# A decode block on one core: the result held on 32 partitions in blocks of 32 columns instead of on 8 partitions in blocks of 128

## The chip, the cores and the metric

The kernel runs on one core of a Trainium2 chip. The metric is the device time of one execution in microseconds (us). Before the change the median of 3 runs is 1310.18 us (1310.18 to 1310.42).

The engines are named as in the profile: PE (TensorE, matrix products; PEld are its loads of the stationary operand), DVE (VectorE), ACT (ScalarE), POOL (GpSimd) and SP (SyncE, which issues most transfers).

## The reference

One token for each of two sequences goes through a layer norm. The result feeds attention over a cache of 32768 keys and values per head (32 query heads on 8 cache heads) and a gated MLP, and both meet in the output:

```python
def reference(A_x, A_k_cache, A_v_cache, A_wq, A_wo, B_x, B_W_gate, B_W_up, B_W_down):
    ...
    x = A_x                                   # (2, 1, 512)
    xn = _layernorm(x, axis=-1)
    s = _A_ref(xn, A_k_cache, A_v_cache, A_wq, A_wo)
    g = _silu(_B_ref(xn, B_W_gate, B_W_up, B_W_down))
    return x + s * g
```

`_A_ref` projects `xn` with `wq` (512 to 32 x 128), takes softmax(q k) v for each head and projects the 4096 values with `wo` back to 512 columns. `_B_ref` is (relu(xn W_gate) * (xn W_up)) W_down, with 1792 inner columns. Everything is float32. The output is 2 rows of 512 numbers; the caches are 2 x 8 x 32768 x 128 numbers each, 537 MB together, and the profile counts 564.67 MB read.

## The kernel before

There are 16 groups, one for each cache head `hk` of each sequence `b`. A group's 32768 keys are 4 tiles of 8192; tiles are handled in pairs, and one transfer brings a pair (8 MB) of keys or values. Keys go to two buffers `k0` and `k1` in turn, values to `wide`. For each tile DVE transposes the keys in place (`k_transpose`, L656), PE makes scores with the keys as the moving operand (`scores`), DVE takes them out of PSUM with their maximum (L674). When a group's four tiles are there, their maximum is found, ACT takes the exponential (L718), PE and DVE turn the weights round, and PE multiplies them with the values (`values`). `finish_group` then brings a group's 4 heads onto partitions: a product with `heads`, a sum over blocks (`ob`, L783), a 32x32-block transpose (`ot`, L791), and a copy on POOL (L794) that puts the four columns of `ot` into `ots[:, hk, :, b * 16]`.

The order of the work is written out by hand: every operation is recorded by `op` with what it reads and writes, waits follow from that, each engine emits its own in the order of recording, and steps 4 to 64 of PE, DVE and ACT stand as a hardware loop. All matrix products share the helper line L241, all transfers L238, so groups are told apart by the names of their tiles. The transfers of the caches are all issued by SP, in one queue; near its end it issues the last values and then `wo` in ten pieces (`load_wo`): one for each of the heads 0 to 6, and for head 7 a half and two quarters (`wo7_0` with products 0 and 1, `wo7_2`, `wo7_3`). `wo` lies in `k1`.

A float32 matmul of the program stands in the trace as two loads and two matmuls. With a stationary operand of 32 columns, a product fills one group of 32 output partitions, and four matmuls for the four groups run side by side; I call that a round.

`project_near` (L802) multiplies heads 0 to 6 with their rows of `wo`: for each head, four matmuls of 512 columns, whose sums land on the four groups of partitions of `near`. DVE copies `near` to `py_sb` (L821). `project_far` (L823) ends the projection with five products into `far`, in the order j = 0, j = 1, the fold, j = 2, j = 3. Those with a j take a quarter of head 7; the fold multiplies `py_sb` with `fold`, a 0/1 matrix that adds up the four groups. Each is four matmuls of 128 columns, one for each quarter `c` of the 512 result columns, which lands on partitions 32c to 32c + 31. Of those partitions the first is sequence 0 and the 17th is sequence 1, as the row of `ots` has it; the others are zeros. So the result is 4 blocks of 128 columns on 8 used partitions. DVE multiplies by `gy` (L846) and adds `xy` (L848), both on 128x128, and SP stores every 16th partition of `gy` with one transfer.

`gy` is written long before by `mlp_fold`, which folds the MLP's result with four such matmuls and applies Silu on ACT (L644). `xy` is a copy of `x` in the same layout, loaded at the start by a transfer that ACT issues after that of `x` itself.

Of the kernel before, what the change touches and what calls it, by code (L numbers as in the profile page):

```python
# [4 lines left out]
AF = mybir.ActivationFunctionType  # L5
# [3 lines left out]
P = 128  # L9
# [4 lines left out]
NEAR = 7  # L14
ALIGN = 512
PERIOD = 4
APART = 16


class Op:  # L20
# [141 lines left out]
def decode_block_kernel(nc, x, kc, vc, wq, wo, wg, wu, wd, out):  # L162
    B, HKV, SK, DH = kc.shape
    D = x.shape[2]
# [13 lines left out]
    pg = Program()  # L178

    def sbuf(name, *shape, align=32):  # L180
        return nc.alloc_sbuf_tensor(name, list(shape), F32, align_bytes=align)[:]

    def bank(name):
        return nc.alloc_psum_tensor(name, [P, 512], F32)[:]
# [5 lines left out]
    os_ = [sbuf(f"os{i}", P, 512) for i in range(2)]  # L190
# [7 lines left out]
    negone = sbuf("negone", 1, 1)  # L198
    eps_t = sbuf("eps_t", 32, 1)
    zero = sbuf("zero", P, 1)  # L200
    xy = sbuf("xy", P, P)
    gy = sbuf("gy", P, P)
    both = sbuf("both", P, B, NC)
    qd = sbuf("qd", P, REP, B, HKV)
    qall = sbuf("qall", P, B, HKV, 4, REP)
    block_of = sbuf("block_of", P, Q)
    qcur = sbuf("qcur", P, 4, Q)
    ots = sbuf("ots", P, HKV, 4, 32)
    heads = sbuf("heads", P, REP, 32)
    fold = sbuf("fold", P, 32)  # L210
    stat = sbuf("stat", 32, 8)
    mx = sbuf("mx", P, NU)
    ls = sbuf("ls", P, NU)
# [6 lines left out]
    ot = sbuf("ot", P, DH)  # L220
# [5 lines left out]
    ps_d = bank("d")  # L226

    def dve(fn, r=(), w=()):
        pg.op("DVE", fn, r, w)

    def act(fn, r=(), w=()):
        pg.op("ACT", fn, r, w)

    def pe(fn, r=(), w=()):
        pg.op("PE", fn, r, w)

    def load(dst, src, sem, r=(), w=(), engine="SP"):
        pg.op(engine, lambda e: e.dma_start(dst, src), r, w, dma=sem)  # L238

    def mm(out_, lhs, rhs, start, stop):  # L240
        return lambda e: e.matmul(out_, lhs, rhs, start=start, stop=stop, skip_group_check=True)  # L241

    def chain(parts):
        def emit(e):
            for f in parts:
                got = f(e)
            return got

        return emit

    def group(g):
        return g % B, g // B
# [6 lines left out]
    load(wide, wq.rearrange("(p k) n -> p (k n)", k=NKC), "wq", w=["wide"])  # L259

    def of_columns(t):
        return t[0:P:APART, :]

    def by_column(t):
        return t.rearrange("b s (c n) -> c (b s) n", c=4)

    pg.op("POOL", lambda e: e.memset(ident, 0.0), (), ["ident"])
    pg.op(
# [17 lines left out]
    dve(lambda e: e.memset(xy, 0.0), w=["xy"])  # L286
    load(xp[0 : B * APART : APART, :], x.rearrange("b s d -> (b s) d"), "xp", w=["st0"], engine="ACT")
    load(of_columns(xy), by_column(x), "xy", w=["xy"], engine="ACT")
    dve(lambda e: e.memset(perm, 0.0), w=["perm"])
    dve(lambda e: e.memset(mrow, 0.0), w=["mrow"])  # L290
# [4 lines left out]
    for kb in range(4):  # L295
        dve(
            lambda e, kb=kb: e.memset(block_of[Q * kb : Q * kb + Q, kb * REP : (kb + 1) * REP], 1.0),
            w=["block_of"],
        )
    dve(lambda e: e.memset(heads, 0.0), w=["heads"])  # L300
    dve(lambda e: e.memset(o_ps, 0.0), w=["o"])
    dve(lambda e: e.memset(ots, 0.0), w=[f"ots{hk}" for hk in range(HKV)])

    dve(
        lambda e: e.tensor_reduce(
# [20 lines left out]
    n = 1  # L326
    while n < Q:
# [18 lines left out]
    dve(  # L346
        lambda e: e.tensor_copy(both, ident.rearrange("p (c k) -> p k c", c=NC)[:, 0 : B * APART : APART, :]),
        ["ident"],
# [5 lines left out]
        ["ident"],  # L354
        ["fold"],
    )

    dve(lambda e: e.reduce_sum(stat[:, 0:1], xp, axis=AX.X), ["st0"], ["stat"])
    dve(lambda e: e.tensor_scalar_mul(stat[:, 1:2], stat[:, 0:1], 1.0 / D), ["stat"], ["stat"])
# [71 lines left out]
    WO, WOK = {}, {}  # L431
# [192 lines left out]

    def mlp_fold():
        dve(lambda e: e.tensor_copy(os_[0], ps_d), ["d"], ["os0"])
        pe(
            chain(
                [
                    mm(  # L630
                        ps_d[32 * c : 32 * c + 32, :P],
                        fold,
                        os_[0][:, c * P : (c + 1) * P],
                        True,
                        True,
                    )
                    for c in range(4)
                ]
            ),
            ["fold", "os0"],  # L640
            ["d"],
        )
        act(
            lambda e: e.activation(gy, ps_d[:, :P], AF.Silu, bias=zero, scale=1.0),  # L644
            ["d", "zero"],
            ["gy"],
        )
# [127 lines left out]
    def finish_group(g):  # L775
        b, hk = group(g)
        pe(
            mm(ps_m[1], heads.rearrange("p h m -> p (h m)"), os_[0], True, True),
            ["heads", "os0"],
            ["m1"],  # L780
        )
        dve(
            lambda e: e.reduce_sum(  # L783
                ob.rearrange("p (j q) -> p q j", j=4),
                ps_m[1].rearrange("p (c q j) -> p q j c", c=NC, j=4),
                axis=AX.X,
            ),
            ["m1"],
            ["ob"],
        )  # L790
        dve(lambda e: e.transpose(ot, ob), ["ob"], ["ot"])  # L791
        pg.op(
            "POOL",
            lambda e: e.tensor_copy(ots[:, hk, :, b * APART], ot.rearrange("p (j m) -> p j m", j=4)[:, :, 0]),  # L794
            ["ot"],
            [f"ots{hk}"],
        )

    near, far = ps_s
    py_sb = os_[0]  # L800

    def project_near(hks):  # L802
        for hk in hks:
            pe(
                chain(
                    [
                        mm(
                            near[32 * j : 32 * j + 32, :],
                            ots[:, hk, j, :],
                            WO[hk][:, j, :],  # L810
                            hk == 0,
                            hk == NEAR - 1,
                        )
                        for j in range(4)
                    ]
                ),
                [f"ots{hk}", WOK[hk][0]],
                ["s0"],
            )
        if hks[-1] == NEAR - 1:  # L820
            dve(lambda e: e.tensor_copy(py_sb, near), ["s0"], ["os0"])  # L821

    def project_far(hks):  # L823
        parts = []
        for hk in hks:
            for j in range(4):
                parts.append((ots[:, hk, j, :], WO[hk][:, j, :], [f"ots{hk}", WOK[hk][j]]))
        parts.insert(2, (fold, py_sb, ["fold", "os0"]))
        for n, (o, w, held) in enumerate(parts):
            pe(  # L830
                chain(
                    [
                        mm(
                            far[32 * c : 32 * c + 32, :P],
                            o,
                            w[:, c * P : (c + 1) * P],
                            n == 0,
                            n == len(parts) - 1,
                        )
                        for c in range(4)  # L840
                    ]
                ),
                held,
                ["s1"],
            )
        dve(lambda e: e.tensor_mul(gy, far[:, :P], gy), ["s1", "gy"], ["gy"])  # L846
        dve(
            lambda e: e.tensor_add(gy, gy, xy),  # L848
            ["gy", "xy"],
            ["gy"],  # L850
        )
# [6 lines left out]
    for j in range(PAIRS + 2):  # L858
        s, v = 2 * j, 2 * (j - 2)
# [22 lines left out]
        if j == 1:  # L882
            mlp_fold()
        if ends:
            if live:
                tile_maximum()
            if summed:
                sums()
            if live:
                maximum()  # L890
            if summed:
                take_o()
                if not live:
                    project_near(range(1))
                finish_group(j // 2 - 1)
# [14 lines left out]
            load_wo()  # L910

    project_near(range(1, NEAR))
    project_far(range(NEAR, HKV))
    load(by_column(out), of_columns(gy), "out", r=["gy"])

    sems = {s: nc.alloc_semaphore(f"sem_{s}") for s in pg.count}
# [55 lines left out]
```

## Time and profile before

| | before |
|---|---|
| median of 3 runs | 1310.18 us |
| the profiled execution | 1310.07 us |
| its span | 1308.4 us |
| mean granted clock of TensorE | 0.833 |
| PE busy | 846.4 us (65%) |
| DVE busy | 706.8 us (54%) |
| moved by DMA | 564.79 MB, mean 432 GB/s |

A row of the timeline has the start and the time taken in us, the engine, the line, the operation, what it writes and reads, the shapes and how many were merged into the row; in brackets stands how long the engine was idle before it and what ended that. Instructions of one row can overlap, so the time of a row is not the sum of its members. A row of the page's groups ends with the busy time in us, the mean of one instruction in ns, and the idle time before them with what ended it.

### The profile page before, as it was taken

How to read it: one execution, taken by the hardware profiler on the slowest of the kernel's cores; microseconds unless marked ns; L12 is line 12 of the kernel's file. 1: busy time of each engine (PE TensorE's matmuls, PEld its weight loads, DVE VectorE, ACT ScalarE, POOL GpSimd, SP SyncE). 2: the span in 40 equal slices, each digit the busy share in tenths (PEclk: the TensorE clock that was granted, in tenths of full speed). 3: DMA queues.
4: the chain of work that ended last, by engine and by line, in shares of the span. 5: the costliest groups of instructions: out<-in, count | busy, mean ns of one | idle time of the engine just before them, and what ended most of it. 6: DMA issues, size and time to landing. Idle time of an engine off the chain costs nothing.

```text
span 1308.4 us, 10823 instructions
## 1 busy us (share of the span) xinstructions
PE 846.4 (65%) x4624; PEld 198.9 (15%) x4624; DVE 706.8 (54%) x642; ACT 51.4 (4%) x133; POOL 10.3 (1%) x38
## 2 busy tenths in 40 slices
PE   3566675675566577556667657666666766765676
PEld 1111111111111111111111111111111111111121
DVE  3566554565655465664546665455665545656521
ACT  0001000000000000000000000000000000000000
POOL 0000000000000000000000000000000000000000
PEclk9678788978878897887898787789877879888788
DMA  9999999999999999999999999999999999999998
GB/s 417 421 434 443 437 427 443 427 437 429 439 427 439 429 439 441 427 443 429 437 429 439 427 439 429 439 441 427 443 429 437 429 439 427 439 429 439 441 427 360
DMA packets 11268, 564.79 MB, mean 432 GB/s; under 512 B 1258, under 2 KB 1274, under 8 KB 1660
## 3 DMA queue, kind: packets, MB, share of 16 engines
q1 hardware_dynamic: 11244, 564.67, 99.7%
q8 instruction: 6, 0.10, 0.0%
q14 instruction: 2, 0.02, 0.0%
q10 hardware_dynamic: 16, 0.01, 0.0%
HBM read 564.67 MB, written 0.00 MB: 432 GB/s over the span
## 4 chain that ended last, share of the span: by engine, by line
DMA 64%; DVE 18%; PE 14%; issue 4%; SPq 0%
DMA k<-in_A_k_cache_dram 59%; DVE k L656 18%; PE o L241 8%; PE s L241 5%; DMA k<-in_A_wo_dram 3%; DMA w<-in_A_wq_dram 2%; PE m_ps L241 1%; SPq L238 0%; PE m_ps L689 0%; DVE gy L846 0%; DVE gy L848 0%
## 5 line engine op out<-in xcount | busy, mean ns | idle before, releaser
L241 PE MATMUL s<-k,qcur 128*32 128x512 f32 x2048 | 497.7, 694 | 398.1 <-DVE k L656 397.7
L656 DVE STREAM_TRANSPOSE k<-k 128x2048 f32<-128x2048 f32 x256 | 565.2, 2275 | 171.4 <-DMA k<-in_A_k_cache_dram 171.4
L241 PE MATMUL o<-w,wt 128*16 128x512 f32 x1984 | 245.3, 596 | 7.4 <-DMA w<-in_A_v_cache_dram 7.4
L241 PEld LDWEIGHTS s<-k,qcur 128*32 128x32 f32 x2048 | 88.3, 121 | 804.7 <-DVE k L656 665.0
L733 DVE STREAM_TRANSPOSE wt<-pt 128x512 f32<-128x512 f32 x64 | 45.4, 709 | 133.0 <-PE pt L241 129.6
L674 DVE TENSOR_SCALAR_CACHE_REDUCE st<-s 128x512 f32<-128x512 f32 x64 | 43.0, 672 | 118.1 <-PE s L241 118.1
L718 ACT ACTIVATE st<-st,nb 128x512 f32<-128x512 f32 x64 | 45.4, 710 | 1110.6 <-DVE nb L715 1110.6
L241 PEld LDWEIGHTS o<-w,wt 128*16 128x16 f32 x1984 | 62.7, 98 | 165.5 <-issue 165.5
L241 PE MATMUL pt<-st,perm 128*128 128x512 f32 x128 | 66.6, 645 | 1.5 <-ACT st L718 1.5
L759 DVE RECIPROCAL rl<-m_ps 128x1 f32<-128x1 f32 x16 | 2.7, 168 | 109.3 <-PE m_ps L241 109.3
L241 PEld LDWEIGHTS pt<-st,perm 128*128 128x128 f32 x128 | 25.0, 206 | 41.4 <-issue 37.2
L241 PE MATMUL m_ps<-os,heads 128*128 128x512 f32 x32 | 20.1, 715 | 13.7 <-DVE os L763 13.7
L783 DVE TENSOR_REDUCE ob<-m_ps 128x128 f32<-128x512 f32 x16 | 11.1, 693 | 21.6 <-PE m_ps L241 21.6
L241 PE MATMUL m_ps<-w,wt 128*32 128x512 f32 (+1 forms) x128 | 16.0, 632 | 7.9 <-DMA w<-in_A_wq_dram 7.9
L526 POOL TENSOR_TENSOR qcur<-qall,block_of 128x128 f32<-128x128 f32 x16 | 6.5, 406 | 1019.0 <-PE s L241 984.8
L241 PE MATMUL o<-k,wt 128*16 128x512 f32 x64 | 10.0, 792 | 4.0 <-DMA k<-in_A_v_cache_dram 4.0
L241 PE MATMUL m_ps<-negone,mrow 1*128 1x1 f32 x32 | 6.0, 256 | 9.3 <-DVE mrow L704 9.3
L718 ACT ACTIVATION_READ_ACCUMULATOR st<-st,nb 128x1 f32 x64 | 11.9, 186 | 0.0
L763 DVE SCALAR_TENSOR_TENSOR os<-o,rl,own 128x512 f32<-128x512 f32 x16 | 11.9, 743 | 0.0
L477 DVE COPY os<-m_ps 128x512 f32<-128x512 f32 x2 | 1.4, 691 | 15.9 <-PE m_ps L241 15.9
L385 PE MATMUL m_ps<-ident,st 32*128 32x32 f32 x4 | 0.7, 307 | 14.2 <-DVE st L374 14.2
L241 PE MATMUL s<-k,ots 128*32 128x512 f32 (+1 forms) x88 | 8.1, 481 | 1.6 <-DMA k<-in_A_wo_dram 1.6
(79 smaller groups left out, 94.9 us busy)
## 6 DMA issues: line engine op xcount, KB each, us to landing
k<-in_A_wo_dram SPq DMA_DIRECT2D x7, 1024.0 KB, 36.2
w<-in_B_W_gate_dram SPq DMA_DIRECT2D x1, 3584.0 KB, 20.0
w<-in_B_W_up_dram SPq DMA_DIRECT2D x1, 3584.0 KB, 28.1
w<-in_B_W_down_dram SPq DMA_DIRECT2D x1, 3584.0 KB, 15.7
k<-in_A_k_cache_dram SPq DMA_DIRECT2D x32, 48.6
k<-in_A_wo_dram SPq DMA_DIRECT2D x1, 512.0 KB, 42.9
k<-in_A_wo_dram SPq DMA_DIRECT2D x2, 256.0 KB, 26.4
w<-in_A_v_cache_dram SPq DMA_DIRECT2D x31, 29.6
```

Of the source, the lines that this page charges most:

```text
L241: return lambda e: e.matmul(out_, lhs, rhs, start=start, stop=stop, skip_group_check=True)
L385: lambda e, k=k: e.transpose(px[:, k * 32 : (k + 1) * 32], xquad[:, k, :], ident[:32, :32])
L477: dve(lambda e, q=qs, h=half: e.tensor_copy(q, pq[h]), [f"m{half}"], [f"os{half}"])
L526: lambda e: e.tensor_tensor(qcur.rearrange("p e (k h) -> p e k h", h=REP), qall[:, b, hk].unsqueeze(2).to_broadcast([P, 4, Q // REP, REP]) ...
L656: dve(lambda e: e.transpose(at_, at_), [f"k{t // 2 % 2}"], [key])
L674: lambda e: e.tensor_scalar(st[u], ps_s[t % 2], SCALE, None, op0=ALU.mult, op1=ALU.max, accum_out=mx[:, u : u + 1],),
L718: lambda e, u=u: e.activation(st[u], st[u], AF.Exp, bias=nb, scale=1.0, accum_out=ls[:, u : u + 1]),
L733: dve(lambda e: e.transpose(wt[t % 2], ps_p[t % 2]), [f"pt{t % 2}"], [f"wt{t % 2}"])
L759: dve(lambda e: e.reciprocal(rl, ps_m[1][:, :1]), ["m1"], ["rl"])
L763: lambda e: e.scalar_tensor_tensor(os_[0].rearrange("p (c d) -> p c d", c=NC), o_ps.rearrange("p (c d) -> p c d", c=NC), rl, own.unsqueeze ...
L783: lambda e: e.reduce_sum(ob.rearrange("p (j q) -> p q j", j=4), ps_m[1].rearrange("p (c q j) -> p q j c", c=NC, j=4), axis=AX.X,),
```

## The change

The result's 512 columns become 16 blocks of 32 (`PARTS`), one on every fourth partition in pairs: block c of sequence b lies on partition 8c + 4b. `xy` and `gy` are 128x32. To get there, each product of the end is 16 matmuls of 32 columns (`spread_mm`): block 4a + i goes to the group a of 32 partitions, with a stationary operand for each i whose used column is 8i + 4b and whose other columns are zero; the four i of a group add up on the same 32x32 field. Those four stationary operands stand in `folds` for the fold and in `last` for head 7, each filled by copies that write one value to four places (`spot`): two on DVE for `folds` at the start, and four on POOL for each of the two groups of head 7 in the place of one. `ots` holds heads 0 to 6 alone. The load of `xy` and the store have 32 runs of 32 numbers where they had 8 of 128.

```diff
+    WIDTH = D // PARTS
+    xy = sbuf("xy", P, WIDTH)
+    gy = sbuf("gy", P, WIDTH)
...
-    ots = sbuf("ots", P, HKV, 4, 32)
+    ots = sbuf("ots", P, HKV - 1, 4, 32)
+    folds = sbuf("folds", P, 4, 32)
+    last = sbuf("last", P, 4, 4, 32)
...
     def of_columns(t):
-        return t[0:P:APART, :]
+        return t[0 : P : P // (B * PARTS), :]
+
+    def spot(t, b):
+        step = P // (B * PARTS)
+        flat_ = t.rearrange("p i m -> p (i m)")
+        return flat_[:, b * step : b * step + 3 * (32 + B * step) + 1 : 32 + B * step]
+
+    def spread_mm(t, lhs, rhs, start, stop):
+        return [
+            mm(
+                t[32 * a : 32 * a + 32, :WIDTH],
+                lhs[:, i, :],
+                rhs[:, (4 * a + i) * WIDTH : (4 * a + i + 1) * WIDTH],
+                start and i == 0,
+                stop and i == 3,
+            )
+            for i in range(4)
+            for a in range(4)
+        ]
 
     def by_column(t):
-        return t.rearrange("b s (c n) -> c (b s) n", c=4)
+        return t.rearrange("b s (c n) -> c (b s) n", c=PARTS)
...
-    dve(lambda e: e.memset(ots, 0.0), w=[f"ots{hk}" for hk in range(HKV)])
+    dve(lambda e: e.memset(ots, 0.0), w=[f"ots{hk}" for hk in range(HKV - 1)])
+    dve(lambda e: e.memset(last, 0.0), w=["last"])
+    dve(lambda e: e.memset(folds, 0.0), w=["folds"])
...
+    for b in range(B):
+        dve(
+            lambda e, b=b: e.tensor_copy(
+                spot(folds, b), fold[:, b * APART : b * APART + 1].to_broadcast([P, 4])
+            ),
+            ["fold"],
+            ["folds"],
+        )
...
     def mlp_fold():
         dve(lambda e: e.tensor_copy(os_[0], ps_d), ["d"], ["os0"])
...
+        pe(chain(spread_mm(ps_d, folds, os_[0], True, True)), ["folds", "os0"], ["d"])
         act(
-            lambda e: e.activation(gy, ps_d[:, :P], AF.Silu, bias=zero, scale=1.0),
+            lambda e: e.activation(gy, ps_d[:, :WIDTH], AF.Silu, bias=zero, scale=1.0),
...
+        row = ot.rearrange("p (j m) -> p j m", j=4)[:, :, 0]
+        if hk < HKV - 1:
...
+        else:
+            for j in range(4):
+                pg.op(
+                    "POOL",
+                    lambda e, j=j: e.tensor_copy(
+                        spot(last[:, j], b), row[:, j : j + 1].to_broadcast([P, 4])
+                    ),
+                    ["ot"],
+                    ["last"],
+                )
...
-    def project_far(hks):
...
+    def project_far():
+        hk = HKV - 1
+        parts = [(last[:, j], WO[hk][:, j, :], ["last", WOK[hk][j]]) for j in range(4)]
+        parts.insert(2, (folds, py_sb, ["folds", "os0"]))
+        for n, (lhs, w, held) in enumerate(parts):
+            pe(chain(spread_mm(far, lhs, w, n == 0, n == len(parts) - 1)), held, ["s1"])
+        dve(lambda e: e.tensor_mul(gy, far[:, :WIDTH], gy), ["s1", "gy"], ["gy"])
```

The end of PE's order shows the five products. The names are the output, the moving operand and the stationary one; the sizes are those of the output. Before:

```order
L241 MATMUL s<-k,ots 32x512 x24
L241 MATMUL s<-k,ots 32x128 x8
L241 MATMUL s<-os,fold 32x128 x4
L241 MATMUL s<-k,ots 32x128 x8
L917 UNCONDITIONAL_BRANCH
```

With the change:

```order
L245 MATMUL s<-k,ots 32x512 x24
L245 MATMUL s<-k,last 32x32 x32
L245 MATMUL s<-os,folds 32x32 x16
L245 MATMUL s<-k,last 32x32 x32
L929 UNCONDITIONAL_BRANCH
```

Of each product's four matmuls there are now sixteen, with a quarter of the columns each, 80 where there were 20; the order of the products stays. POOL's order ends, before:

```order
L526 TENSOR_TENSOR qcur<-qall,block_of 128x128
L794 COPY ots<-ot 128x4 x3
L917 UNCONDITIONAL_BRANCH
L941 ISA
```

and with the change:

```order
L813 COPY ots<-ot 128x4
L821 COPY last<-ot 128x4 x8
L929 UNCONDITIONAL_BRANCH
L953 ISA
```

The last two of the sixteen copies of `ot` have become eight.

More of the change, by code (lines that the diff above doesn't have):

```diff
@@ L17 @@
 APART = 16
+PARTS = 16
 class Op:
@@ L200, in decode_block_kernel @@
     zero = sbuf("zero", P, 1)
-    xy = sbuf("xy", P, P)
-    gy = sbuf("gy", P, P)
+    WIDTH = D // PARTS
+    xy = sbuf("xy", P, WIDTH)
+    gy = sbuf("gy", P, WIDTH)
     both = sbuf("both", P, B, NC)
@@ L626, in mlp_fold @@
         dve(lambda e: e.tensor_copy(os_[0], ps_d), ["d"], ["os0"])
[L627 to L642, printed above, removed]
+        pe(chain(spread_mm(ps_d, folds, os_[0], True, True)), ["folds", "os0"], ["d"])
         act(
-            lambda e: e.activation(gy, ps_d[:, :P], AF.Silu, bias=zero, scale=1.0),
+            lambda e: e.activation(gy, ps_d[:, :WIDTH], AF.Silu, bias=zero, scale=1.0),
             ["d", "zero"],
@@ L791, in finish_group @@
         dve(lambda e: e.transpose(ot, ob), ["ob"], ["ot"])
[L792 to L797, printed above, removed]
+        row = ot.rearrange("p (j m) -> p j m", j=4)[:, :, 0]
+        if hk < HKV - 1:
+            pg.op(
+                "POOL",
+                lambda e: e.tensor_copy(ots[:, hk, :, b * APART], row),
+                ["ot"],
+                [f"ots{hk}"],
+            )
+        else:
+            for j in range(4):
+                pg.op(
+                    "POOL",
+                    lambda e, j=j: e.tensor_copy(
+                        spot(last[:, j], b), row[:, j : j + 1].to_broadcast([P, 4])
+                    ),
+                    ["ot"],
+                    ["last"],
+                )
     near, far = ps_s
@@ L821, in project_near @@
             dve(lambda e: e.tensor_copy(py_sb, near), ["s0"], ["os0"])
-    def project_far(hks):
[L824 to L846, printed above, removed]
+    def project_far():
[5 more added lines that the diff above has]
+        dve(lambda e: e.tensor_mul(gy, far[:, :WIDTH], gy), ["s1", "gy"], ["gy"])
         dve(
@@ L912, in decode_block_kernel @@
     project_near(range(1, NEAR))
-    project_far(range(NEAR, HKV))
+    project_far()
     load(by_column(out), of_columns(gy), "out", r=["gy"])
```

## The prediction

> **What bounds the kernel now.** I read the page first, for what limits the whole span.
>
> ```profile
> span 1308.4 us, 10823 instructions
> PE 846.4 (65%) x4624; PEld 198.9 (15%) x4624; DVE 706.8 (54%) x642; ACT 51.4 (4%) x133; POOL 10.3 (1%) x38
> DMA  9999999999999999999999999999999999999998
> GB/s 417 421 434 443 437 427 443 427 437 429 439 427 439 429 439 441 427 443 429 437 429 439 427 439 429 439 441 427 443 429 437 429 439 427 439 429 439 441 427 360
> q8 instruction: 6, 0.10, 0.0%
> DMA 64%; DVE 18%; PE 14%; issue 4%; SPq 0%
> L241 PE MATMUL s<-k,qcur 128*32 128x512 f32 x2048 | 497.7, 694 | 398.1 <-DVE k L656 397.7
> L241 PEld LDWEIGHTS s<-k,qcur 128*32 128x32 f32 x2048 | 88.3, 121 | 804.7 <-DVE k L656 665.0
> L241 PEld LDWEIGHTS o<-w,wt 128*16 128x16 f32 x1984 | 62.7, 98 | 165.5 <-issue 165.5
> L241 PEld LDWEIGHTS pt<-st,perm 128*128 128x128 f32 x128 | 25.0, 206 | 41.4 <-issue 37.2
> ```
>
> The reader is to see that the transfers are busy in every slice but the last, at 417 to 443 GB/s. Nothing the change does there touches a transfer of the caches, so only what stands behind the last transfer, or holds one up, can move the end. PE has 398 us in which it waits for the transposed keys: work added to it in the middle falls into that. Then I read the timeline of the end, after the last pieces of `wo` have been asked for, and the chain of waits over the same stretch.
>
> ```profile
> 1261.28 42.93 DMA k<-in_A_wo_dram
> ...
> 1304.35 1.62 PE s L241 x40
> ...
> ```
>
> ```profile
> 1304.15 0.69 DVE L821 COPY os<-s 128x512 f32<-128x512 f32 x1 [5.73 <-PE s L241]
> 1304.32 0.41 PEld L241 LDWEIGHTS s<-k,ots 128*32 128x32 f32 x16 [1.15 <-issue]
> 1304.35 0.65 PE L241 MATMUL s<-k,ots 128*32 128x128 f32 x16 [0.27 <-DMA k<-in_A_wo_dram]
> 1304.89 0.16 PEld L241 LDWEIGHTS s<-os,fold 128*32 128x32 f32 x8 [0.17 <-DVE os L821]
> 1304.89 0.42 PE L241 MATMUL s<-os,fold 128*32 128x128 f32 x8
> 1305.03 0.24 PEld L241 LDWEIGHTS s<-k,ots 128*32 128x32 f32 x8
> 1305.13 0.79 PE L241 MATMUL s<-k,ots 128*32 128x128 f32 x16
> 1305.50 0.16 PEld L241 LDWEIGHTS s<-k,ots 128*32 128x32 f32 x8 [0.23 <-DMA k<-in_A_wo_dram]
> 1305.99 0.29 DVE L846 TENSOR_TENSOR gy<-s,gy 128x128 f32<-128x128 f32 x1 [1.15 <-PE s L241]
> 1306.32 0.29 DVE L848 TENSOR_TENSOR gy<-gy,xy 128x128 f32<-128x128 f32 x1
> 1306.64 0.69 SPq L238 DMA_DIRECT2D out_dram<-gy  x1
> ```
>
> The end is a relay. The last piece of `wo` lets PE start at 1305.50; PE is done at 1305.13 + 0.79 = 1305.92; DVE multiplies and adds until 1306.61; the store is issued at 1306.64 and the span ends at 1308.4, 1.76 us later. Within this, three waits matter: the first piece of the last head (1304.32), DVE's copy of the near sum (1304.89), and the last piece (1305.50). A matmul of the program stands as two loads and two matmuls in these rows (x8 for the fold's four), so PE goes through five products of 8, 40 in all, and each product is two rounds of four, one for each group of 32 output partitions.
>
> **The change part by part.** DVE: L846 and L848 go from 128 columns to 32.
>
> ```profile
> 11.74 0.68 DVE L365 TENSOR_TENSOR st<-st 32x512 f32<-32x512 f32 x1
> 1295.13 0.17 DVE L759 RECIPROCAL rl<-m_ps 128x1 f32<-128x1 f32 x1 [15.84 <-PE m_ps L241]
> ```
>
> 512 columns take 0.68 us and 128 take 0.29: 0.39 / 384 = 1.0 ns a column. So 96 columns less are 0.097 us, twice that 0.19. The floor is not reached: a single column out of PSUM takes 0.17, and 0.29 - 0.10 = 0.19 is still above. By that floor the two can give between 0.19 and at most 0.24; I take **-0.19**. It is on the path in full, since the store waits for it.
>
> PE at the end: each product becomes 8 rounds of four (16 matmuls, two passes) with 32 moving columns, where it was 2 rounds with 128. The moving columns per group of partitions are the same in all, so the question is what one short round costs. Three bounds from rows:
>
> ```profile
> 1297.65 0.13 PEld L241 LDWEIGHTS s<-k,ots 128*32 128x32 f32 x4 [0.30 <-issue]
> 1298.08 0.13 PEld L241 LDWEIGHTS s<-k,ots 128*32 128x32 f32 x4 [0.30 <-issue]
> 31.68 1.95 PE L241 MATMUL pt<-both,os 128*128 128x8 f32 x16
> 1295.00:1303.00 8.00, 6.65 (x51) 1.66 (x51) 1.93 (x4) 0.00 (x0) 0.19 (x1) 1.00 1.00 419
> 1303.00:1308.40 5.40, 2.64 (x48) 1.09 (x48) 1.28 (x3) 0.00 (x0) 0.00 (x0) 1.00 0.24 93
> ```
>
> Streaming: rounds of 512 columns follow each other by 0.43 us, so 32 columns stream in 0.027. The loads of the weights run under it (each set of four starts with the round before). Loading: with 8 moving columns and 128 columns of weights, 16 pairs take 1.95, (1.95 - 0.26) / 15 = 0.113 each, so the load sets the pace there; mean loads of 98, 121 and 206 ns for 16, 32 and 128 columns give about 1 ns a column, so 32 columns are about 0.031. Issue: the fold's eight loads take 0.16 in all with about 0.11 each, so they start within 0.05, some 7 ns apart with the matmuls between them; four pairs need 0.027. The last two rows are stretches of the end, whose columns after the interval are the time busy of PE, its loads, DVE, ACT and POOL, then the granted clock (1.00), the share of DMA and GB/s: no throttle enters. The greatest of the three is 0.031 a round. The last product is then 8 x 0.031 = 0.25 where it is 0.22: **+0.03**. The products ahead of it: 16 rounds from 1304.35 are over by 1304.85, before the fold may start (1304.89); 16 more from there by 1305.39, before the last piece (1305.50). That cover is good up to (1305.50 - 1304.89) / 16 = 0.038 a round; above it PE, not the last transfer, is late. Below, a round cannot be cheaper than 0.027, which gives +0.00. Above, nothing in the trace runs pairs denser than four per 0.11, and that end is rival one.
>
> The Trainium skill speaks against this edit. "TensorEngine Tiling (Array Packing)", section Performance Considerations (Instruction Overhead), has a matmul of few moving columns cost as much as one of 60, some 60 cycles, and says not to take the tiling out of a dimension that is already small. If the floor holds for each group of columns by itself, its 25 ns at 2.4 GHz lie under the 27 ns of the stream and change nothing; rows 7 ns apart agree with that. If it held across the groups, 160 x 25 ns = 4.0 us would stand where 40 short rounds do, the result of rival one within half a microsecond.
>
> The store has 32 runs of 128 bytes where it had 8 of 512.
>
> ```profile
> 0.74 0.39 SPq L238 DMA_DIRECT2D w<-in_A_wq_dram  x1
> 2.65 0.60 ACTq L238 DMA_DIRECT2D xy<-in_A_x_dram  x1
> w<-in_A_wq_dram SPq DMA_DIRECT2D x1, 21.9
> ```
>
> Its issue took 0.69, the load of `xy`, which has the same shape, 0.60, and a load over 128 partitions 0.39. If more partitions make the issue that much shorter, the store ends 0.30 sooner. On the other side, the 8.39 MB of `wq` landed 21.9 us after issue; at 432 GB/s they move in 19.4, so a transfer over all partitions has up to 2.5 us around its data, 0.7 more than the store's 1.76. The nearest row is the store itself (same queue, same 4 KB): I take **0.00**, between -0.30 and +0.7. "DMA: Bandwidth & Descriptors" of the skill, section Specifications, has writes under 512 bytes read and modify memory first, which speaks for the dear end; no run shown here has such a store.
>
> Edits that I cost at nothing, with their cover:
>
> ```profile
> 1298.48 0.19 POOL L794 COPY ots<-ot 128x4 f32<-128x4 f32 x1 [36.28 <-DVE ot L791]
> 10.35 0.67 DVE L358 TENSOR_REDUCE stat<-st 32x1 f32<-32x512 f32 x1 [3.54 <-DMA st<-in_A_x_dram]
> 2.74 0.48 DVE L301 MEMSET o<- 128x512 f32 x1
> ```
>
> The last head's row goes out as four POOL copies, one after the other: 4 x 0.19 and a wait between, under 2 us from 1298.48, needed at 1304.32; without cover 0.6 or so. At the start DVE gets one more such memset of 128x512, one of a quarter of that, and two copies of four columns: less than 1.2 if each of these three costs a half of the 0.48, before a wait of 3.54 for `x`. The fold of the second block, near 102 us, is 8 rounds for 2: at 0.109 each +0.65, in the stretch where PE waits for keys. The load of `xy` on ACT's queue is read first by work that waits for far later transfers.
>
> Sum: -0.19 + 0.03 + 0.00 = **-0.16 us**. The profiled execution took 1310.07 (span 1308.4 and 1.67 around it), so 1309.91; it lies 0.11 under the median of the runs, so I forecast 1310.0.
>
> **The rivals.** One, on the other side: short pairs go no faster than the densest that the trace shows, four per 0.109. PE then needs 40 rounds from 1304.35; the last starts at 1304.35 + 39 x 0.109 = 1308.60 and ends 0.28 later, 2.96 us after today's 1305.92. Less DVE's 0.19 that is +2.77: 1312.9. It decides from 0.038 a round. For it: no row has shorter rounds, and nowhere does a group of partitions get its next weights so soon. Against it: loads start 7 ns apart, and the pace of every long round is explained by its columns. A milder form has loads and streams one after the other, 0.027 + 0.027 = 0.055: last start 1306.50, end 1306.78, +0.86 - 0.19 = +0.67: 1310.8.
>
> Two: the store is dearer by up to 0.7, or the longer code hurts: 72 more matmuls of four instructions each, and the page has six instruction packets of 0.10 MB, 16 KB each; one that falls on a DMA engine with the last piece holds it for 16 KB / (432 / 16 GB/s) = 0.6 us. Either way 1310.6 or so.
>
> Three: the store over more partitions is issued sooner: -0.16 - 0.30, 1309.7.
>
> Four: the change does not do what it says, if DVE's operations have a floor near today's 0.29. The 0.17 of a single column speaks against it; the time would be 1310.2.
>
> **How the numbers follow.** Forecast 0.50, rival one 0.10 and its milder form 0.13, two 0.13, three 0.11, four 0.03. The range takes in three at its low end with 0.3 for a median's scatter, and rival two and the mild form at the high end: 1309.4 to 1311.3; left out are rival one and the outer parts of the others. A fifth of a percent, 2.6 us, is about what a measurement of this kernel can tell from no change: rival one lies at that bound, so slower gets 0.06 of its 0.10, and 0.02 for a hold-up that I have not seen; no case gains 2.6 us, so faster 0.02; within, 0.90.
>
> **What would show it.** Right: L846's and L848's successors at 0.19 each and 0.2 us less between PE's end and the store's issue; short rounds 0.03 apart, so that PE still waits for the last piece of `wo` before its last 32 loads. Wrong: the last product's loads starting late with no transfer as their releaser (rival one), a longer stretch from the store's issue to the span's end (two), a last piece that lands late beside an added instruction packet, or a first scores row that comes later than before, where the start was not hidden.

## The result and the profile after

| | before | changed |
|---|---|---|
| median of 22 runs each | 1310.21 us (1310.01 to 1310.57) | 1312.13 us (1311.80 to 1312.59) |
| ratio | | 1.0015, 95% interval 1.0009 to 1.0021 |
| profiled execution, its span | 1310.07 and 1308.4 us | 1311.80 and 1310.3 us |
| mean granted clock | 0.833 | 0.836 |

The change costs 1.9 us; the forecast was 1310.0, with 1309.4 to 1311.3 as the range. These are the rows of the changed kernel's timeline at the end, from the first piece of `wo` for head 7 on:

```profile
1304.32 0.67 PEld L245 LDWEIGHTS s<-k,last 128*32 128x32 f32 x64 [1.19 <-issue]
1304.35 0.74 PE L245 MATMUL s<-k,last 128*32 128x32 f32 x63 [0.31 <-DMA k<-in_A_wo_dram]
1304.89 0.39 PEld L245 LDWEIGHTS s<-os,folds 128*32 128x32 f32 x32
...
1305.19 0.68 PEld L245 LDWEIGHTS s<-k,last 128*32 128x32 f32 x64
...
1305.21 0.76 PE L245 MATMUL s<-k,last 128*32 128x32 f32 x62
1307.79 0.19 PE L245 MATMUL s<-k,last 128*32 128x32 f32 x1 [1.83 <-issue]
1308.02 0.19 DVE L858 TENSOR_TENSOR gy<-s,gy 128x32 f32<-128x32 f32 x1 [3.23 <-PE s L245]
1308.24 0.19 DVE L860 TENSOR_TENSOR gy<-gy,xy 128x32 f32<-128x32 f32 x1
1308.46 0.66 SPq L242 DMA_DIRECT2D out_dram<-gy  x1
```

The 80 matmuls of the program at the end are 160 in the trace. All but one of them are through by 1305.21 + 0.76 = 1305.97, as the forecast has it. The last one alone starts at 1307.79. Its weights are loaded (the 64 loads end at 1305.87), its piece of `wo` was there for the 31 before it, and the trace knows no semaphore that it waited for: `issue`. The chain of waits over the same stretch says the same, and its 1.83 us of `issue` are the only wait that the chain before does not have:

```profile
1304.35 1.62 PE s L245 x108
1305.96 1.83 issue
1307.79 0.20 PE s L245
1308.00 0.02 issue
1308.02 0.20 DVE gy L858
```

The sum from the two timelines: PE ends at 1307.98 where it ended at 1305.92, +2.06. From there to the store's issue it is 0.48 where it was 0.72, -0.24. From the issue to the span's end 1.84 where it was 1.76, +0.08. Together +1.90, the span's difference.

What the last matmul lacks shows in the page's list of DMA queues, where the queue q8 carries instructions. The changed kernel has

```profile
q8 instruction: 7, 0.11, 0.0%
q10 hardware_dynamic: 52, 0.01, 0.0%
```

where the kernel before has six packets. Each is 16 KB. Their places in time are in the trace, though no row of a view prints them; these are the last ones of q8, in us from the span's start, with the time that the packet took:

```
before   1293.07  0.96
after    1289.30  0.88
after    1305.36  0.93
```

The seventh packet starts while PE is in its last products and is moved by 1306.28; the last matmul goes 1.5 us later. That the packet holds the last matmul's code is so far a guess from this order in time; the experiments test it.

### The profile page after: what moved, and what is told of

Its sections match the earlier page's. It is cut to its first block, busy times and chain, and to the rows that moved or that the text cites. A ratio compares the mean times of both kernels' runs of the same rounds, so it can differ in the third digit from the quotient of the medians.

```text
span 1310.3 us, 11121 instructions
## 1 busy us (share of the span) xinstructions
PE 843.9 (64%) x4768; PEld 199.5 (15%) x4768; DVE 707.2 (54%) x646; ACT 51.3 (4%) x133; POOL 11.4 (1%) x44
## 4 chain that ended last, share of the span: by engine, by line
DMA 63%; DVE 18%; PE 14%; issue 4%; SPq 0%
DMA k<-in_A_k_cache_dram 58%; DVE k L673 18%; PE o L245 8%; PE s L245 5%; DMA k<-in_A_wo_dram 3%; DMA w<-in_A_wq_dram 2%; PE m_ps L245 1%; SPq L242 0%; PE m_ps L706 0%; DVE gy L858 0%; DVE gy L860 0%
## 5 line engine op out<-in xcount | busy, mean ns | idle before, releaser
L245 PEld LDWEIGHTS m_ps<-w,wt 128*32 128x32 f32 x128 | 5.9, 123 | 17.1 <-issue 17.1
```

## The experiments

The theory A from this: PE runs code out of blocks of 16 KB, and asks for one more when it enters a block. The products at the end are 160 pairs of load and matmul; a block holds 128 pairs. The last matmul is the first instruction of a block, the request for it goes out only in the first two products, and the 128 pairs ahead of it are through in 1.4 us. "Runtime: NRT & Kernel Launch" of the Trainium skill, section "Instruction fetch mechanics", describes such blocks, of 16 KiB or 256 instructions, and calls the cost of crossing into one mostly hidden; the packets here have that size, and the cost is not hidden.

The rivals: B, the array or PSUM holds back the last short matmul; C, each instruction more costs; and, after the first four runs, D, a boundary near the end costs its 2 us whatever runs ahead of it. To move the boundaries and nothing else at the end, matmuls are added to (or one is taken from) PE's code long before, near 100 us, where PE waits for keys. Each matmul is two pairs, so n of them move every later boundary by 2n pairs.

**e1: one matmul less.**

```diff
-                    for i in range(FI)
+                    for i in range(FI) if i != 5
```

> The changed kernel, with one of the 14 matmuls of the MLP's down projection left out (its part of the inner columns is missing from the result), near 90 us. The end of the program is as in the changed kernel; all of PE's code behind that place moves four instructions towards the start. Theory A (the last matmul's code comes late: it is the first instruction of a 16 KB block that PE's sequencer asks for only when it enters the block before, and the 128 pairs of that block are gone through faster than the block arrives): the last matmul falls into the block before, its idle time of 1.83 us is gone, PE ends near 1306.0, time 1310.1. Rival B (the last matmul waits for something in the array or PSUM: a drain of the short rounds, the sums that pile up on one field): nothing at the end differs, so 1312.1 with the same idle time. Rival C (every instruction more costs): 4 of 288 less, 1312.1.

Measured: 1309.99 us (1309.83 to 1310.24, 11 runs; before 1310.14 beside it). The end of its timeline:

```profile
1305.60 0.68 PEld L245 LDWEIGHTS s<-k,last 128*32 128x32 f32 x64
...
1305.62 0.77 PE L245 MATMUL s<-k,last 128*32 128x32 f32 x63
1306.46 0.19 DVE L858 TENSOR_TENSOR gy<-s,gy 128x32 f32<-128x32 f32 x1 [1.25 <-PE s L245]
```

The end has the same instructions on the same data paths, and the last matmul is no longer late. B falls: four instructions that were left out 1200 us earlier cannot change what the array does at the end. C falls as well, since 4 of 288 instructions took 2.1 us with them.

**e2, e3, e4: 8, 16 and 24 matmuls more.** The MLP's fold repeats itself; the sums written first are overwritten. The diff is e2's; e3, e4 and later e5, e6, e9 and e10 have another number in the place of 8.

```diff
-        pe(chain(spread_mm(ps_d, folds, os_[0], True, True)), ["folds", "os0"], ["d"])
+        once = spread_mm(ps_d, folds, os_[0], True, True)
+        pe(chain((once + once)[:8] + once), ["folds", "os0"], ["d"])
```

> The changed kernel, with the MLP's fold made longer by 8 matmuls whose sums are written over at once (near 102 us, result unchanged). The end of the program is the same; its code lies 16 pairs further on. Theory A: 16 pairs of the last product and the last matmul stand in the late block, which is asked for about 15 pairs after the start of the five products instead of 31, 0.1 us sooner; the rest then takes 17 pairs x 0.008 and the idle time shrinks little: between 1312.0 and 1312.3, with the idle time now ahead of a group of about 17 pairs. Rival B: 1312.1, idle before the last matmul alone. Rival C: 1312.2.

> As before with 16 matmuls more in the MLP's fold (result unchanged). Theory A: the block is entered with the last pair of head 6, which waits for its piece of wo at 1303.0 instead of 1304.45; 3.3 us later, at 1306.3, its first instruction can go, 33 pairs follow: PE ends near 1306.8, time about 1310.9. Rival B: 1312.1. Rival C: 1312.3.

> As before with 24 matmuls more in the MLP's fold (result unchanged). Theory A: the block is entered within head 5 or sooner, near 1301, so it is there by 1304.4 and nothing waits for it: no idle time but that for the last piece of wo, 1310.1, with 96 instructions more than the changed kernel. Rival B: 1312.1. Rival C: 1312.4 or more.

Measured: e2 1312.18 us (1311.83 to 1312.64), e3 1312.97 (1311.11 to 1313.48), e4 1309.98 (1309.80 to 1310.34), 11 runs each. The place of the wait, in e2's timeline and then in e3's:

```profile
1305.26 0.62 PE L245 MATMUL s<-k,last 128*32 128x32 f32 x46
1308.09 0.34 PE L245 MATMUL s<-k,last 128*32 128x32 f32 x17 [2.21 <-issue]
```

```profile
1305.46 0.46 PE L245 MATMUL s<-k,last 128*32 128x32 f32 x30
1307.88 0.46 PE L245 MATMUL s<-k,last 128*32 128x32 f32 x33 [1.95 <-issue]
```

The reader is to see x17 and x33 behind the wait where the changed kernel has x1: two pairs for each matmul added, exact. The wait sits on a place of the code, not on a piece of work. In e4 there is none:

```profile
1304.68 0.74 PE L245 MATMUL s<-k,last 128*32 128x32 f32 x63 [0.46 <-DMA k<-in_A_wo_dram]
...
1305.54 0.77 PE L245 MATMUL s<-k,last 128*32 128x32 f32 x63
1306.38 0.19 DVE L859 TENSOR_TENSOR gy<-s,gy 128x32 f32<-128x32 f32 x1 [1.39 <-PE s L245]
```

Its packet of instructions starts at 1301.76, and 96 instructions more than in the changed kernel make it 2 us faster. e3 missed its number: 3 of 11 runs lie at 1311.1 to 1311.2, near the 1310.9 expected, and 8 at 1312.6 to 1313.5. The near ones are partly luck: their spans are 1308.9 to 1309.1, about 0.6 us above the median of e6's, 1308.4, and the rest is the 2.0 to 2.2 us that these executions took outside the span, where e6's took about 1.5. In the profiled one, a long one, the packet starts at 1305.48, not near 1304.

**e5: 18 more, to get a wait of half the length.**

> As e3, with 18 matmuls more in the MLP's fold (result unchanged). Theory A, with what e1 to e4 showed (some 3.4 us from the entry into a block to the first instruction of the next one): the block is entered in the middle of head 6's matmuls, which wait for their piece of wo until about 1303.1. The next block's first instruction can go near 1306.5; 37 pairs and the pipeline follow, PE ends near 1307.0, one us later than without a wait: 1311.0, in every run, between the changed kernel's 1312.1 and e4's 1310.0. Rival D (a block boundary anywhere in the last stretch costs its 2 us whole, or nothing): 1312.2 or 1310.0.

Measured: 1312.51 us, again in two clumps: 3 of 11 runs at 1310.5 to 1310.9, 8 at 1312.2 to 1313.0. The profiled one, a long one, has x37 behind a wait of 2.27 us, as counted, and its packet starts at 1305.68. Only the short executions come near the 1311.0 expected; neither A as written nor D tells why there are two kinds.

**e6: 40 more, the best version.**

> The changed kernel with 40 matmuls more in the MLP's fold (result unchanged). Theory A: the block that holds the last 81 pairs is asked for at the entry into the one before, 209 pairs from the end, near 1295; nothing waits, and 160 instructions more near 102 us cost nothing: 1310.0, no idle time of PE in the last products but that for the last piece of wo.

Measured: 1309.94 us (1309.85 to 1310.17, 11 runs) beside 1310.15 (1309.95 to 1310.48, 33 runs) of the kernel before; ratio 0.9999 with an interval of 0.9990 to 1.0008, so the comparison itself does not set the two apart. The packet starts at 1296.55, with the entry expected near 1295. The end of its timeline:

```profile
1305.18 0.68 PEld L245 LDWEIGHTS s<-k,last 128*32 128x32 f32 x64
...
1305.20 0.77 PE L245 MATMUL s<-k,last 128*32 128x32 f32 x63
1306.04 0.19 DVE L859 TENSOR_TENSOR gy<-s,gy 128x32 f32<-128x32 f32 x1 [1.19 <-PE s L245]
1306.27 0.19 DVE L861 TENSOR_TENSOR gy<-gy,xy 128x32 f32<-128x32 f32 x1
1306.48 0.66 SPq L242 DMA_DIRECT2D out_dram<-gy  x1
```

**e7: the kernel before, with its last matmul moved to the start of a block, by the count of instructions.**

```diff
-                    for c in range(4)
+                    for c in (0, 1, 2, 3) * 3
```

> The kernel before, with its MLP fold done three times (8 matmuls more, result unchanged). By the count of instructions its last matmul then stands first in its block, as in the changed kernel. Theory A: the block before it holds 128 pairs of which the last 40 alone are the far products, so it is entered near 1293 and the last block is there 10 us before its use: 1310.2, no idle time ahead of the last matmul. Rival D: 1312.1.

Measured: 1310.20 us (1310.05 to 1310.91), the kernel before beside it 1310.15. The last products follow their piece of `wo` as in the kernel before:

```profile
1305.21 0.77 PE L241 MATMUL s<-k,ots 128*32 128x128 f32 x16
1305.56 0.16 PEld L241 LDWEIGHTS s<-k,ots 128*32 128x32 f32 x8 [0.21 <-DMA k<-in_A_wo_dram]
```

Its last packets start at 1289.84 and at 1305.87. The kernel before has none after 1293.07, so here PE entered one more block near its end; that this block begins with the very last matmul rests on the count alone. D falls: a boundary at the end costs nothing where the 128 pairs ahead of the last matmul, counted back from the end, take some 14 us.

**e8: half as far, 8 blocks of 64 columns.**

```diff
-PARTS = 16
+PARTS = 8
```

The helpers' numbers of four follow it (`PARTS // 4` fields to a group).

> The change with 8 blocks of 64 columns on 16 partitions: 8 matmuls of 64 columns a product. DVE's last two operations at 0.23 each, 0.13 less together; rounds of 0.055; the store has 16 runs of 256 bytes. By the count of instructions the last block starts 32 pairs before the end and the one before is entered near 1294. Theory A: nothing late, 1310.0 to 1310.1. Rival C (what counts is the number of matmuls): 1310.9.

Measured: 1310.16 us (1310.05 to 1310.49), the kernel before 1310.15. DVE's two operations take 0.22 each, no wait of PE for its code. So A holds to within 0.1 us and C, with 1310.9, does not. The packets that had to be there in time started at 1289.84 in e7 and at 1291.66 in e8, where the expectations had the blocks entered near 1293 and 1294, so the count tells the time of a request to some 3 us and not better. In the profiled execution the store is issued 0.58 us after PE's end, where it was 0.72 before, as expected; the medians do not show this 0.14, which is less than the runs of one kernel scatter.

**e9 to e12: when is a block asked for?**

> As e5, with 20 matmuls more in the MLP's fold (result unchanged): the block before the last is entered exactly with head 6's first matmul. What e5 left open is when the block is asked for. If the request goes out while the sequencer stands at that matmul's wait (head 5 is issued by 1301.5), the last block is there by 1305 and the time is 1310.0. If it goes out with the matmul itself (1303.1 to 1303.4) and the 3.4 us stand, 1311.0. If a request of that time is held up until the last pieces of wo have landed (1305.4), 1312.3, as in most executions of e5.

> As e5, with 17 matmuls more (result unchanged): the block is entered four instructions before the five products. If the request goes out on entry and takes as long as in e5's short executions, 1311.0; if it is held up until wo has landed, 1312.4; a mixture of the two as in e3 and e5 if the two are close.

> e5 again for one look. Where this execution is one of the short ones (about 3 of 11), its packet of 16 KB of instructions starts before 1305 and PE's idle time before the last block is about 0.5 us; where it is a long one, after 1305.3 and 2.2 us.

> e3 again for one look, with the same reading as e11: a short execution has its packet of instructions before 1305, a long one after 1305.3.

Measured: e9 1312.59 us (2 of 10 runs at 1310.5 to 1310.6, the others at 1312.3 or more), e10 1312.24 (4 of 10 at 1310.2 to 1310.8), e11 1312.19, e12 1310.66. In e9 the third of the expected cases came in most executions and the first, 1310.0, in none; e10 is the expected mixture. e11 is a long execution with its packet after 1305.3 and e12 a short one with its packet before 1305, as expected; their waits, 1.97 and 0.23 us, are some 0.25 shorter than expected. e12 has this in its timeline:

```profile
1305.47 1.06 PE L245 MATMUL s<-k,last 128*32 128x32 f32 x63
1306.08 0.35 PEld L245 LDWEIGHTS s<-k,last 128*32 128x32 f32 x32 [0.23 <-issue]
```

From the traces, the start of the packet that brings the last block, the first instruction out of that block, and the wait ahead of it:

```
                        packet   first instruction   wait of PE or its loads
after                   1305.36   1307.79              1.83
e2                      1305.43   1308.09              2.21
e3                      1305.48   1307.88              1.95
e5                      1305.68   1308.33              2.27
e9                      1305.77   1308.13              2.57
e10                     1306.04   1308.40              2.40
e11                     1305.44   1307.82              1.97
e12                     1303.82   1306.07              0.23
```

The same code as e3's waits 0.23 us in e12, where the packet started 1.66 sooner. From the packet's start to the first instruction it takes 2.2 to 2.7 us in every row. PE is busy with the block before for some of it, and waits for the rest: that is what a late block costs. When the request goes out is not settled. For blocks entered with head 6 or right ahead of the five products (e3, e5, e9, e10, e11, e12) the packet starts either 0.6 us after head 6's start, in e12, the one short execution that was profiled, or 0.9 to 1.5 us after the first of the five, and executions of one kernel differ. The traces add one thing: in every row but e12's the packet starts after the last packet of `wo` has ended, by 0.06 to 0.64 us (e3 1305.48 after 1305.42, e11 1305.44 after 1305.37, e9 1305.77 after 1305.13). That fits a request held up until `wo` has landed, the third case of e9. It is no fixed rule, though: e12's packet at 1303.82 and e4's at 1301.76 started while `wo` was still being moved. For the changed kernel and e2, whose blocks are entered near 1304.6, a plain delay of 0.8 us fits as well. No run changed the transfers of `wo` to tell the two apart.

## Why the prediction was wrong

By its steps, against e6, which has the change without the late block:

- DVE, forecast -0.19: from PE's end to the store's issue 1306.48 - 1305.97 = 0.51, where it was 0.72: -0.21. Right, with 0.19 for each operation as said.
- PE's short rounds, forecast +0.03 at 0.031 a round: PE ends at 1305.97 where it ended at 1305.92, +0.05. In the changed kernel the fold's 32 loads take 0.39 with 0.108 each, so its 8 rounds lie (0.39 - 0.11) / 7.75 = 0.036 apart, under the 0.038 from which PE would have been late, though not by much. One sign that the prediction named for being right is missing: PE no longer waits for the last piece of `wo`. Its last 64 loads run through without idle time (e6, 1305.18 and 0.68), and the last 32 of them start near 1305.47, where the kernel before was released by the transfer at 1305.50. The cover is all but used up. Rival one, with 0.109, is off by a factor of three. The floor that "TensorEngine Tiling (Array Packing)" of the Trainium skill, section Performance Considerations, sets for short matmuls, taken across the groups of columns, does not show in this trace: 63 matmuls take 0.74 in all, 12 ns each.
- The store, forecast 0.00: from its issue to the span's end 1.84 where it was 1.76, +0.08, as in the changed kernel (the ends taken from the traces, e6's at 1308.33). The issue takes 0.66 where it took 0.69, so rival three's cheaper issue did not come, nor did rival two's dear store.
- The edits costed at nothing: the four POOL copies took 0.94 in all, from 1298.86, and the start still has a wait of 2.58 us for `x` where it had 3.54. Their cover held.
- The sum, -0.16: e6 against the kernel before beside it is 1309.94 - 1310.15 = -0.21. The parts above add up to -0.08, which is the difference of the two profiled spans; both lie within the interval of the comparison, and so does no difference. Within what the runs can tell, the working of the forecast gives the time of a version whose code is there in time.

The step that failed is the one in which rival two dealt with the longer code: "one that falls on a DMA engine with the last piece holds it for 16 KB / (432 / 16 GB/s) = 0.6 us". The packets were seen and counted, but priced as traffic that a data transfer meets, 0.6 us at most, and left out of the sum. That hold-up did not come: the added packet starts at 1305.36, after the last of `wo` had landed at 1305.16. What the runs show in its place is that PE itself has to wait for the packet's contents: 2.2 to 2.7 us from its start, of which 1.83 were left over in the changed kernel. The page before had the numbers for it: 4624 matmuls and as many loads in code with a loop, and packets of 16 KB. The working asked how fast pairs can be issued and took their supply for granted; 80 matmuls where 20 were are four times the code in the same time.

## What to carry to other kernels

A stretch of code that runs through more than one 16 KB block of instructions in a few microseconds can wait for its own code, and the profile shows that as idle time of PE with `issue` as its releaser in the middle of a product that has all its data. Splitting matmuls finer multiplies code as well as rounds; count the pairs of load and matmul at the end of a kernel, 128 to a block, and ask when the block before the last is entered. Padding or trimming PE's code near 100 us moved the boundary here, and 40 matmuls more in that place, where PE waits for keys, cost nothing that the runs show.

## What was not expected of the hardware

A kernel's time moved by 2 us with one matmul left out 1200 us before its end (1312.13 to 1309.99), and as far the same way with 40 more (1309.94). Kernels whose block is asked for within a few instructions of a wait have two times, 1310.5 and 1312.5 in e5, with the same code and the same data. All 11 executions of e3 took 2.0 to 2.6 us outside their spans, where e6's took about 1.5. The profiled one has one more packet of instructions after the span's end, at 1312.2, but so have e5, e9, e10 and e11 (1311.4 to 1312.0), whose profiled executions took 1.4 to 1.7, so the packet does not explain it and the cause is open. In e4's trace a packet of instructions (1306.61 to 1307.91) runs beside the store, and the span ends 2.21 us after the store's issue, where it is 1.84 or 1.85 in the other runs with 16 blocks. That may be a hold-up as in rival two, on the store; it is one execution, and e4's median (1309.98) does not show it.
